# A list schedule rebuilt: new durations with margins, 22 activation groups, work moved to VectorE, identity products in TensorE's early waits, the last tile by rows

## The chip, the cores and the metric

One core of one Trainium2 chip. The metric is the device time of the slowest (here the only) core in microseconds. Every comparison below is between executions that were put in the fast state; executions of one kernel scatter by 2 to 4 us to either side of their median (the kernel before: 530.85 to 536.88 us in 63 runs on one chip), and its medians on the chips used here lie between 532.2 and 533.0 us. So ratios are always taken against the kernel before on the same chip in the same rounds.

## The reference, cut to what matters

```python
# 4 sequences of 5824 steps, 256 channels: a gated linear recurrence ...
a_t   = exp(8 * sigmoid(r_gate) * log(sigmoid(a_param)))
x_in  = sqrt(max(1 - a_t*a_t, 1e-6)) * sigmoid(i_gate) * x
h     = a_t[:, t] * h + x_in[:, t]          # over t, y[:, t] = h
# ... and on its 23296 rows a multiplicative feed-forward net (w3: 1024 x 1024)
out   = ((y @ w1) * (y @ w2)) @ w3 @ w_out
```

## The kernel before

The rows are cut into chunks: one of 256, then 45 of 512. Per chunk, ScalarE takes tanh of both gates, the decay's exp and a square root; the gates are turned by TensorE (first chunks) or by transposing DMAs; GpSimd and VectorE make products and squares; VectorE scans; then four pairs of "up" tiles (pa, pb) on TensorE, a copy of pa by ScalarE, the product g by VectorE, four "down" tiles, a copy out and a store. w3 and w_out are folded into one matrix wp at the start. Square root needs another activation table than tanh and exp, so chunks are taken in groups: all roots of a group stand together.

The order of instructions is not written by hand. A list scheduler in the kernel's own Python gives every piece of work (a job) an engine, a duration, a due date and buffers, lets time run, and each time an engine is free picks the ready job with the earliest due date. Only the resulting order reaches the chip: each engine executes its instructions strictly in that order.

```python
group_sizes = [2, 2, 2, 3, 3, 4, 4, 4, 4, 3, 4, 2, 5, 4]
NPE, NDV, NCV = 6, 4, 8      # chunks turned by TensorE; products, squares by VectorE; casts by VectorE
WCE = {'w1': 'POOL', 'w2': 'POOL', 'wo': 'POOL', 'w3': 'DVE'}     # who casts the weights
BACKLOG = 0.5                # bulk loads wait while more than this many us of DMA are queued
DUE_W, DUE_W3, LAG = -4.0, 20.5, 21.5                              # ... and a dozen more due dates

def copy(c, mp):   nc.scalar.copy(out=sa, in_=T["pa", c, mp])       # cut
def evac(c, j2):   nc.scalar.copy(out=T["ot", c, j2], in_=T["po", c, j2])
def root(c):       nc.scalar.activation(out=n, in_=n, func=AF.Sqrt, scale=-1.0, bias=1.0)

job(("copy", c, mp), "ACT", 0.15 + 0.82 * f, t + 0.9, ...)          # engine, duration, due date
BUFS = {"pab": 3, "po": 2, "g": 3, "sa": 3, "rt": 2, "th_r": 2, ...}

while any(waiting.values()):                                        # cut
    for e in free:
        key = choose(e, t)        # first ready job of this engine by due date
        ...
        done[key] = end; order.append((start, len(order), key))
for _, _, key in sorted(order):
    jobs[key]["fn"]()             # emit in the order of the planned starts
```

## Time and profile before

| | before |
|---|---|
| time, median of 3 (range) | 532.49 us (532.16 to 533.09) |
| span of the profiled execution | 530.9 us |
| busy: TensorE, VectorE, ScalarE, GpSimd | 498.4, 446.7, 463.1, 335.8 us |
| activation table loads | 31 |
| end of TensorE's work to end of the span | 4.2 us |

TensorE is the engine to look at, and its own work doesn't change with the schedule, so what a schedule does to the time is read from TensorE's *lost* time. The prediction below counts it from blocks. For comparisons I count it in one way for all kernels: TensorE loads weights for every tile and all these loads are in the trace, in order. From one tile's first weight load to the next I subtract the tile's work (0.867 us for a full up, down or fold product tile, 0.445 for eight transposes; halves for chunk 0; 488.6 in all, the identity products counting as nothing). What remains is lost. For the kernel before that gives 34.0 us lost by 84.7 us and 38.1 in all. The prediction's block count splits the same 38.0 as 36.2 and 1.8. That split is wrong: it counts up tiles by their copies and products, which come later than the tiles. By the matmuls' own starts, 28 full up tiles and not 26 began before 84.7 us, so 34.6 us were lost before and 3.5 after; the sum is the same.

### The profile page before, as it was taken

What the parts mean: (1) busy time and instruction counts of PE and PEld (TensorE: products, weight loads), DVE (VectorE), ACT (ScalarE), POOL (GpSimd) and SP (SyncE); (2) the same over time, 40 slices, a digit from 0 to 9 for tenths busy, and PEclk for the clock granted to TensorE, in tenths of its full rate; (3) what the DMA queues carried; (4) which work ended last, traced back from release to release, by engine and by line L of the source; (5) the groups of instructions that cost most, each with busy time, mean ns of one, the idle gap of its engine ahead of it and who ended that gap; (6) DMA issues with size and microseconds to landing.
All of it is one profiled execution on the core that took longest, in us unless ns stands there. A gap on an engine that the chain in (4) does not pass through costs nothing.

```text
span 530.9 us, 8667 instructions
## 1 busy us (share of the span) xinstructions
PE 498.4 (94%) x3144; PEld 303.3 (57%) x3144; DVE 446.7 (84%) x367; ACT 463.1 (87%) x546; POOL 335.8 (63%) x260
## 2 busy tenths in 40 slices
PE   1568899999999999999999999999999999999997
PEld 1434565666565566565656565565665655566655
DVE  2998988997968899998999988789898889899641
ACT  6998879999999999999999899799998999965452
POOL 1338485887758686876859788578868578841000
PEclk9999999999999999999999999999999999999999
DMA  8998999999997996997997879999899787231112
GB/s 274 356 359 243 292 282 296 324 299 275 295 273 199 279 315 171 278 299 197 287 252 221 226 204 238 329 196 266 226 274 303 199 208 212 61 98 59 41 61 99
DMA packets 184939, 124.31 MB, mean 234 GB/s; under 512 B 88640, under 2 KB 182848, under 8 KB 184896
## 3 DMA queue, kind: packets, MB, share of 16 engines
q1 hardware_dynamic: 184624, 123.76, 86.4%
q8 instruction: 24, 0.39, 0.3%
q14 instruction: 19, 0.16, 0.1%
q10 hardware_dynamic: 272, 0.00, 0.0%
HBM read 78.91 MB, written 23.86 MB: 194 GB/s over the span
## 4 chain that ended last, share of the span: by engine, by line
PE 81%; DVE 8%; ACT 4%; issue 3%; DMA 3%; SPq 0%; DVEq 0%; ACTq 0%
PE pa L227 27%; PE pb L227 26%; PE po L248 26%; DVE g_t L241 2%; DMA rt<-th_r 2%; DVE h_t L211 2%; DVE w_t L276 1%; ACT sa L234 1%; PE pw L299 1%; ACT th_i L133 1%; DMA i_t<-in_i_gate_dram 1%; DVE nrm L196 1%; DVE u_t L148 1%; ACT ot L254 1%; ACT a_t L179 1%
## 5 line engine op out<-in xcount | busy, mean ns | idle before, releaser
L241 DVE TENSOR_TENSOR g_t<-sa,pb 128x1024 bf16<-128x1024 bf16 (+1 forms) x184 | 218.4, 1199 | 60.0 <-ACT sa L234 44.8
L227 PEld LDWEIGHTS <-w_sb 128*128 128x128 bf16 x1472 | 144.6, 98 | 149.1 <-issue 10.7
L234 ACT CAST sa<-pa 128x1024 bf16<-128x1024 f32 (+1 forms) x184 | 183.0, 999 | 32.8 <-PE pa L227 30.9
L227 PE MATMUL pa<-y_t,w_sb 128*128 128x512 bf16 (+1 forms) x736 | 188.7, 380 | 4.0 <-DVE g_t L241 4.0
L227 PE MATMUL pb<-y_t,w_sb 128*128 128x512 bf16 (+1 forms) x736 | 188.4, 379 | 2.9 <-DVE g_t L241 1.5
L248 PE MATMUL po<-wp_sb,g_t 128*128 128x256 bf16 x1456 | 181.7, 273 | 0.2 <-DVE nrm L196 0.2
L248 PEld LDWEIGHTS <-g_t 128*128 128x128 bf16 x1456 | 142.4, 98 | 46.0 <-issue 0.4
L211 DVE TENSOR_TENSOR_SCAN h_t<-a_t,h_t,nrm 128x512 f32<-128x512 f32 (+3 forms) x90 | 136.6, 1534 | 0.8
L187 POOL TENSOR_TENSOR nrm<-a_t 128x512 f32<-128x512 f32 x84 | 104.7, 1258 | 43.5 <-ACT a_t L179 43.2
L153 POOL TENSOR_TENSOR u_t<-th_i,x_t 128x512 bf16<-128x512 f32 x80 | 116.5, 1472 | 2.5
L219 POOL CAST y_t<-h_t 128x1024 bf16<-128x1024 f32 x38 | 44.6, 1173 | 67.9 <-DVE h_t L211 62.1
L138 POOL TENSOR_SCALAR th_i<-th_i 128x1024 f32<-128x1024 f32 x42 | 57.6, 1371 | 21.8 <-ACT th_i L133 21.8
L254 ACT COPY ot<-po 128x512 f32<-128x512 f32 x91 | 53.4, 587 | 16.3 <-PE po L248 15.6
L179 ACT ACTIVATE a_t<-rt,la 128x512 f32<-128x512 bf16 x80 | 63.5, 816 | 4.5 <-DMA rt<-th_r 4.2
L196 DVE SCALAR_TENSOR_TENSOR nrm<-nrm,ut 128x1024 f32<-128x1024 f32 x40 | 59.8, 1494 | 2.4 <-ACT nrm L191 2.4
L133 ACT ACTIVATE th_i<-i_t 128x1024 f32<-128x1024 f32 (+1 forms) x46 | 48.2, 1052 | 1.1 <-DMA i_t<-in_i_gate_dram 1.0
L191 ACT ACTIVATE nrm<-nrm 128x1024 f32<-128x1024 f32 (+1 forms) x46 | 48.1, 1056 | 0.8 <-DVE nrm L187 0.6
L126 ACT ACTIVATE th_r<-r_t 128x1024 bf16<-128x1024 f32 x40 | 42.3, 1063 | 2.1 <-DMA r_t<-in_r_gate_dram 2.0
L161 PE MATMUL ptr<-ident,th_r 128*128 128x128 bf16 x44 | 4.7, 269 | 16.7 <-DVE ident L73 8.7
L276 POOL CAST w_sb<-wf 128x1024 bf16<-128x1024 f32 x4 | 6.1, 1545 | 19.7 <-DMA wf<-in_moe_w_dram 19.7
L191 ACT ACT_TABLE_LOAD x14 | 18.0, 1283 | 0.2
L161 PEld LDWEIGHTS <-th_r 128*128 128x128 bf16 x44 | 3.7, 122 | 18.5 <-ACT th_r L124 14.9
(33 smaller groups left out, 127.1 us busy)
## 6 DMA issues: line engine op xcount, KB each, us to landing
out_dram<-ot SPq DMA_DIRECT2D x91, 256.0 KB, 3.6
r_t<-in_r_gate_dram SPq DMA_DIRECT2D x45, 512.0 KB, 5.3
i_t<-in_i_gate_dram SPq DMA_DIRECT2D x45, 512.0 KB, 5.2
x_t<-in_x_dram SPq DMA_DIRECT2D x45, 512.0 KB, 5.0
wf<-in_moe_w_dram SPq DMA_DIRECT2D x12, 512.0 KB, 5.7
wf<-in_moe_w_out_dram SPq DMA_DIRECT2D x2, 512.0 KB, 6.0
rt<-th_r SPq DMA_TRANSPOSE x40, 4.5
ut<-u_t SPq DMA_TRANSPOSE x40, 4.6
```

Source lines behind the costliest of these rows:

```text
L138: nc.gpsimd.tensor_scalar(t, t, 1.0, 1.0, op0=ALU.add, op1=ALU.mult)
L153: nc.gpsimd.tensor_mul(out=u.rearrange("p cb j q -> p j cb q")[:, js], in0=cut(t)[:, js], in1=cut(T["x", c])[:, js])
L179: nc.scalar.activation(out=T["a", c][:, cb, :w], in_=T["pr", c][:, cb, :w], func=AF.Exp, scale=la4[:, cb:cb + 1], bias=la4[:, cb:cb + 1])
L187: eng.tensor_mul(out=T["n", c][:, cb, :w], in0=T["a", c][:, cb, :w], in1=T["a", c][:, cb, :w])
L191: nc.scalar.activation(out=T["n", c][:, :, :w], in_=T["n", c][:, :, :w], func=AF.Sqrt, scale=-1.0, bias=1.0)
L196: nc.vector.scalar_tensor_tensor(out=T["n", c][:, :, :w], in0=T["n", c][:, :, :w], scalar=1e-3, in1=T["pu", c][:, :, :w], op0=ALU.max, op1 ...
L211: nc.vector.tensor_tensor_scan(T["h", c][:, cb, lo:hi], T["a", c][:, cb, lo:hi], T["n", c][:, cb, lo:hi], init, ALU.mult, ALU.add)
L227: nc.tensor.matmul(out=pp[:, q, :w], lhsT=w_sb[:, cb, m * P:(m + 1) * P], rhs=T["y", c][:, cb, :w], start=(cb == 0), stop=(cb == NCB - 1))
L234: nc.scalar.copy(out=sa[:, :, :w], in_=T["pa", c, mp][:, :, :w])
L241: nc.vector.tensor_mul(out=T["g", c][:, 2 * mp:2 * mp + 2, :w], in0=T["sa", c, mp][:, :, :w], in1=T["pb", c, mp][:, :, :w])
L248: nc.tensor.matmul(out=T["po", c, j // 2][:, j % 2, :], lhsT=T["g", c][:, k, j * P:(j + 1) * P], rhs=wp_sb[:, k, :], start=(k == 0), stop= ...
L254: nc.scalar.copy(out=T["ot", c, j2], in_=T["po", c, j2])
```

## The change

Its intent: replace the due dates by a schedule searched on durations recorded on the chip, with a margin added to each, so that the order also holds when jobs are late; let smaller groups shorten the lead; give VectorE some of ScalarE's copies; use TensorE's early waits for products with the identity matrix, whose results nobody reads, to bring its clock up; and shorten the tail. The arithmetic and all buffers stay. Cut to its core:

```diff
-    group_sizes = [2, 2, 2, 3, 3, 4, 4, 4, 4, 3, 4, 2, 5, 4]
+    group_sizes = [2, 1, 1, 2, 3, 3, 2, 3, 2, 1, 1, 2, 5, 3, 3, 1, 2, 3, 2, 2, 1, 1]
-    NPE = 6 ; NDV = 4 ; NCV = 8
+    TURN_R = {0, 1, 2, 3, 5, 6, 10} ; TURN_U = {0, 1, 2, 3, 4}
+    DV_TIMES = {0, 1, 3, 4} ; DV_SQUARE = {0, 1, 3, 4, 5} ; DV_CAST = {2, 3, 4, 7, 10, 11, 13}
+    DV_EVAC = {1, 7, 14, 15, 16, 18, 21, 25, 30, 32, 33, 35, 42, 43, 44}
+    DV_COPY = {4, 16, 18, 19, 20, 23, 25, 29, 32, 33, 34, 42, 43, 44}
-    WCE = {'w1': 'POOL', 'w2': 'POOL', 'wo': 'POOL', 'w3': 'DVE'}
+    W_CAST = {"w1": "DVE", "w2": "POOL", "wo": "POOL", "w3": "POOL"}
-    BACKLOG = 0.5
+    BACKLOG = 1.75
+    M_OCC, M_LAT, M_PE = 0.06, 0.038, 0.0055          # margins on every job
+    OFFSET = {"r": -20.0, "i": -7.5, ...} ; SHIFT = {("w3", 0): 36.0, ...}   # some 240 due dates, chunks 0 to 13
 def up(c, mp, nm, w_sb):
+        for _ in range(warm.get((nm, c, mp), 0)):
+            nc.tensor.matmul(out=pp[:, 0, :P], lhsT=ident, rhs=ident, start=True, stop=True)
 def copy / evac:
+        copy_to(mp == 0 and c in DV_COPY, ...)   /   copy_to(c in DV_EVAC, ...)
 def down(c, j):
+        if c == NCH - 1:
+            T["po_last", j] = po = psum_o.tile([P, D], F32, name="po", tag="po")   # then evac_last, store_last per row tile
 ...
-                job(("copy", c, mp), "ACT", 0.15 + 0.82 * f, t + 0.9, ...)
+                job(("copy", c, mp), e, o + s * f, o + s * f + (0.115 if e == "DVE" else 0.15), t + 0.9, ...)
 ...
+            if key[0] in ("pa", "pb") and t < WARM and t - free[e] > 0.25:
+                n = int((t - free[e]) * 0.8 / 0.0556)
+                if n > 3:
+                    warm[key] = min(n, 60)
```

## The prediction

> **What bounds the kernel now.** I read the page's busy shares first, then the busy times of every engine in eight stretches, the groups of instructions in the two stretches that matter, the waits, and last the order in time of the first and last 30 us.
>
> ```profile
> span 530.9 us, 8667 instructions
> PE 498.4 (94%) x3144; PEld 303.3 (57%) x3144; DVE 446.7 (84%) x367; ACT 463.1 (87%) x546; POOL 335.8 (63%) x260
> 0.00:20.70 20.70, 3.85 (x32) 3.26 (x33) 10.30 (x15) 15.92 (x19) 3.98 (x8) 1.00 0.94 301
> 20.70:84.70 64.00, 54.95 (x395) 34.01 (x393) 58.81 (x58) 55.07 (x69) 40.99 (x32) 0.97 1.01 303
> 84.70:200.00 115.30, 114.93 (x710) 69.47 (x710) 102.06 (x80) 110.64 (x132) 82.82 (x63) 1.00 1.06 281
> 460.00:519.00 59.00, 58.98 (x361) 35.27 (x361) 43.72 (x36) 32.58 (x38) 11.78 (x10) 1.00 0.20 60
> ```
>
> In the last four lines the columns are the stretch, its length, the busy us of PE, PEld, DVE, ACT and POOL, the granted clock, DMA share and GB/s. TensorE is full from 84.7 us on; only the first 85 us are not. But a matmul's end is modelled, so I count work instead. In the steady part a block (four products of 512 columns for an up tile, or eight of 256 for a down tile) starts every 0.867 us: in the order of time, three of them (pa, pb, po) repeat every 2.60 us up to 519. From 84.7 us to the last product's start plus its share (526.8) the groups of that stretch hold 167 copies of pa, 167 products and 87 output copies, so 167+167+174 = 508 blocks, 508 x 0.8667 = 440.3 us in 442.1 us. Only **1.8 us are lost in the last 442 us**; no schedule can take more than that from there.
>
> Before 84.7 us TensorE did: chunk 0's eight half tiles 3.5; 26 full up tiles 22.5; 8 down tiles 6.9; the weight fold, 8 x (0.44+0.87) = 10.5; 12 transposes at 0.445 (half for chunk 0) 5.1. Sum 48.5 us. So **36.2 of the first 84.7 us are lost**, and 4.1 after the last matmul (526.8 to 530.9). Floor of pure work: 48.5+440.3 = 488.8; check: 488.8+36.2+1.8+4.1 = 530.9.
>
> ```profile
> 8.72 0.59 PE L161 MATMUL ptr<-ident,th_r 128*128 128x128 bf16 x4 [8.72 <-DVE ident L73]
> 19.91 1.03 PE L161 MATMUL ptr<-ident,th_r 128*128 128x128 bf16 x8 [4.96 <-ACT th_r L124]
> 20.73 1.06 PE L227 MATMUL pa<-y_t,w_sb 128*128 128x256 bf16 x4
> 29.31 0.60 PE L227 MATMUL pa<-y_t,w_sb 128*128 128x256 bf16 x4
> 37.67 1.86 PE L227 MATMUL pa<-y_t,w_sb 128*128 128x512 bf16 x4 [1.70 <-DVE g_t L241]
> ```
>
> Columns: start, length, engine, line, what it does, count, idle time before and its releaser. The same four products take 1.06 us at 20.73 and 0.60 at 29.31, and the 512-wide ones 1.86 at 37.67 against 1.03 later: TensorE is at half speed after its long waits. By the starts of the following tiles I put this at 3.5 us in all. So the 36.2 us are: 18.9 before the first up tile (20.7 less 1.8 of transposes), 3.5 of half speed, 13.8 of waits from 20.7 to 84.7.
>
> In that ramp VectorE is 58.81 of 64.0 us busy and ScalarE 55.07: together they are the limit, not DMA latency (few DMA waits of ScalarE are in it), and not TensorE.
>
> ```profile
> L241 DVE TENSOR_TENSOR g_t<-sa,pb 128x1024 bf16<-128x1024 bf16 x180 | 215.7, 1210 | 59.9 <-ACT sa L234 44.8 <-PE pb L227 10.3 <-ACT ot L254 2.1
> ...
> L234 ACT CAST sa<-pa 128x1024 bf16<-128x1024 f32 x180 | 180.8, 1009 | 32.6 <-PE pa L227 30.8 <-DVE g_t L241 0.5
> ...
> L211 DVE TENSOR_TENSOR_SCAN h_t<-a_t,h_t,nrm 128x512 f32<-128x512 f32 x84 | 130.1, 1566 | 0.7
> ...
> L254 ACT COPY ot<-po 128x512 f32<-128x512 f32 x91 | 53.4, 587 | 16.3 <-PE po L248 15.6
> ...
> L191 ACT ACT_TABLE_LOAD x14 | 18.0, 1283 | 0.2
> ...
> L276 DVE CAST w_t<-wf 128x1024 bf16<-128x1024 f32 x8 | 8.7, 1105 | 0.0
> ```
>
> After the bar: busy us, mean ns of one, then the idle time before and its releasers. The 60 us that VectorE waits at g_t lie where TensorE is full: they are slack, not loss.
>
> **What the Trainium skill says.** "TensorE: Matmul & The Clock Gate", section "What's actually happening": half clock after an idle window, full clock after about 3.4 us of sustained work. The trace agrees in kind: 0.85 us between starts of the 256-wide tiles at 20.7, 0.43 at 29.3. "ScalarE: Activation LUTs", section "Table sets: the hidden batching unit": tanh and exp share a set, sqrt needs another; the trace has 31 loads of 1283 ns for 14 groups, two per group and three at the start (14+7+6+3+1 in the groups). "SBUF — State Buffer", section "SBUF: two separate sides": VectorE with two SBUF inputs and GpSimd exclude each other for a whole instruction. The trace agrees: the scan takes 1566 ns on average, and 1277 in the last 46 us where GpSimd has little left. So moving work to GpSimd is not free for VectorE's scans and gates.
>
> **The change, part by part.**
>
> 1. Schedule. The arithmetic is the same; the due dates, groups and engine of each job change. TensorE's 488.8 us stay (12 transposes before: 6+6; after: 7+5).
> ScalarE: 15 chunks' output copies go to VectorE, 30 x 0.587 = -17.6; 14 pa copies go, 14 x 1.009 = -14.1; 22 groups in place of 14, two loads each, 16 x 1.283 = +20.5. Net -11, to about 452 us.
> VectorE: 30 output copies at an estimated 0.6 (half the width of the 1.21 product), +18; 14 copies at about 1.2, +17; w3 casts to GpSimd, -8.7; two w1 casts, +1.4; one more chunk of squares, +2.3; casts nearly even. Net about +30, to about 476 us.
> None of this gives TensorE time after 84.7; it only makes VectorE tighter (476 in a span near 520 is 92%).
>
> 2. The ramp, where the gain is. VectorE loses there the w3 casts (-8.7) and the casts of chunks 0, 1, 5 and 6 (0.42 + 3 x 0.69 = -2.5) and gains w1 casts (1.4), squares (2.3), chunk 1's output copies and chunk 4's copy (2.4): -5.1. ScalarE: by 84.7 the old order had tanh done for chunks 0 to 9 with up tiles only into chunk 4, a lead of nearly six chunks, because whole groups of 2, 2, 2, 3 must pass the square root together. A chunk of lead costs ScalarE 2 x 1.06 + 2 x 0.8 + 1.06 = 4.8 us. Groups 2, 1, 1, 2, 3 need perhaps two chunks less by then: -9.6, less one more pair of loads (+2.6) : -7. Both engines are thus relieved by 5 to 7 us, and the 5 and 9 us that they idle in the ramp can be cut by better order. I take 8 of the 13.8 us of waits.
>
> 3. Start. The identity's cast is queued first, and chunk 0's transpose needs no longer wait for it until 8.72. But ScalarE has hardly a gap from 4.5 to 16.4 (tanh, rates, three table loads, exp, then the root of the first group, still two chunks), so the first root stays near 15. The old order then put chunk 1's gate (18.21) ahead of chunk 0's scan result being cast (19.33) and a cold transpose (19.91) ahead of the first up tile. I take 1.5 us, first up tile near 19.2. The preloaded log set replaces a load that was there anyway: 0.
>
> 4. Identity products. Up to 60 in a planned wait over 0.25 us in the first 80 us, filling 80% of it at 0.0556 us each, the full-speed spacing. They bring TensorE to full speed: of the 3.5 us I take 2.5. At half speed they last twice as long (0.107), so a filled wait can overrun by 0.6 of itself; and where the wait is for a PSUM buffer, they too wait for it and come on top. I take 0.5 us back for that, inside the 8 above.
>
> 5. Last tile by rows. Its copy of 256 columns (0.38, as wp's copy from pw) instead of 0.58, and a store of half the size, estimated 0.3 less: -0.5 of the 4.1.
>
> Sum: first part 36.2-8-1.5-2.5 = 24.2; middle 1.8 to 3 (tighter VectorE, more groups); end 3.6. Span 488.8+24.2+3.0+3.6 = 519.6. The time is 1.6 above the span (532.49 against 530.9): **521.2 us**, 2.1% less. As a search over hundreds of due dates probably finds some more than my averages, I put it at **520.5 us**.
>
> **The rivals.**
> - VectorE becomes the bound in the middle. For it: +30 us, scans stretched by GpSimd, three pab buffers only, so a late product stops TensorE within two tiles. Against it: 60 us of slack at g_t, and output and pa copies are given to it where the plan saw room. If half of the chunks cost 0.3 us each, +7: about 527.
> - The ramp stays bound by ScalarE (more table loads among the first chunks) and only the order changes: 3 us in place of 8, so about 526, within 2%.
> - The plan comes out nearly as meant: it gives 11 of the 13.8 us of waits back, first up tile at 18, middle as clean as before. Then about 514.
> - Identity products overrun in several waits: +2 to +4 on any of these.
>
> **Range and chances.** 8 in 10: 512 to 527. The threshold of 2% is 521.8 us, just above my figure, so the chances are close: faster 0.58, same 0.39, slower 0.03. Slower would need more than 10 us of new stalls in a kernel that loses 42 in all, with the schedule chosen to withstand delays.
>
> **What would show it.** First up tile near 19 us; TensorE's full stretch beginning near 70 to 75 instead of 85; lost time before it near 24 us; no 1.8 us up tile in the first 60 us; under 4 us lost after it; VectorE near 476 and ScalarE near 452 us busy, 47 table loads; 3.6 us from last matmul to end. I am wrong if TensorE's waits on g_t or sa spread through 100 to 460 us, if the first up tile is still at 20.7, or if the products with the identity stand ahead of up tiles whose input had long been ready.

## The result, and the profile after

The changed kernel took **537.31 us** (536.72 to 539.00, 4 runs) beside 532.79 us for the kernel before: a ratio of 1.009, 95% interval 1.0061 to 1.0118. So it is not 2.3% faster but 0.9% slower, outside my range of 512 to 527. (A ratio is the mean time of one kernel's fast runs over that of the other's of the same rounds, so not quite the ratio of the medians that I quote.) The profiled execution was the slowest of the four; a second study of the same kernel, told below, gave 1.013.

From the page of the changed kernel (span 537.2 us): busy time and share of each engine, and the shares of the chain that ended last; after it the same chain line of the kernel before.

```profile
PE 500.6 (93%) x3165; PEld 309.2 (58%) x3221; DVE 472.6 (88%) x408; ACT 450.1 (84%) x515; POOL 353.2 (66%) x265
...
PE 60%; ACT 14%; DMA 11%; issue 7%; DVE 7%; SPq 1%; POOL 0%; ACTq 0%; DVEq 0%; POOLq 0%
```

```profile
PE 81%; DVE 8%; ACT 4%; issue 3%; DMA 3%; SPq 0%; DVEq 0%; ACTq 0%
```

The busy times are nearly what I had worked out (VectorE 476 forecast, 472.6 measured; ScalarE 452 and 450.1). What they did to TensorE is not. Of the chain that ends the kernel, TensorE's share fell from 81% to 60%: ScalarE and DMA took its place.

Now the ramp. Busy time by engine (PE, PEld, DVE, ACT, POOL) in three stretches, then the granted clock, DMA share and GB/s; the kernel before first, then the changed one.

```profile
20.00:40.00 20.00, 15.84 (x102) 9.49 (x103) 19.77 (x20) 18.66 (x23) 7.67 (x7) 0.94 1.08 361
40.00:60.00 20.00, 16.55 (x132) 10.10 (x131) 18.55 (x19) 17.04 (x21) 12.89 (x11) 0.98 0.89 276
60.00:80.00 20.00, 18.85 (x144) 12.59 (x142) 17.94 (x17) 15.38 (x21) 15.81 (x13) 1.00 1.04 269
```

```profile
20.00:40.00 20.00, 18.97 (x157) 13.67 (x157) 18.39 (x19) 18.87 (x23) 12.27 (x12) 1.00 1.09 356
40.00:60.00 20.00, 18.08 (x157) 12.11 (x159) 19.76 (x20) 15.45 (x22) 11.11 (x10) 1.00 1.15 299
60.00:80.00 20.00, 13.74 (x106) 9.86 (x106) 14.91 (x14) 18.03 (x22) 17.13 (x12) 0.91 1.11 325
```

Up to 60 us the new order is ahead (identity products swell its PE figures, so go by lost time: 28.0 us against 31.5). From 60 to 80 us it gives back more than it had won: TensorE is busy 13.74 us instead of 18.85, and the lost time grows by 8.8 us against 2.0. The chain of work in that stretch shows one part of it (start, length, what):

```profile
51.99 6.87 DMA rt<-th_r
...
58.88 1.53 ACT a_t L246 x2
...
61.87 1.28 ACT L263
...
63.17 1.07 ACT nrm L263
...
68.12 1.33 DVE nrm L268
69.45 1.99 DVE h_t L283
...
71.46 1.35 DVE y_t L291
72.81 1.97 DVE h_t L283
74.78 0.59 DVE ot L308
...
75.42 2.64 PE po L333 x12
```

A transposed th_r lands after 6.87 us, exp waits for it, then a table load and the root, then gates, scans and a cast on VectorE in a row, and only behind them, in VectorE's queue, an output copy that frees the buffer which a down tile needs. In this execution the moved output copy put TensorE behind VectorE's longest jobs. The down tiles after the wait ran at half speed besides (16 products from 75.42 us on took 3.49 us; 16 took 1.91 in the kernel before).

The chain leaves out another wait in the same stretch. The change also gave the w3 casts to GpSimd, and TensorE waited for them. Its waits (us in all, how many, the longest) in this profile, then in the second one of the same kernel, told below:

```profile
PE ptw L379 <- POOL w_t L370: 3.1, 3, 2.1
PE po L333 <- DVE ot L308: 2.7, 1, 2.7
```

```profile
PE ptw L379 <- POOL w_t L370: 4.2, 4, 2.1
PE po L333 <- DVE ot L308: 0.6, 1, 0.6
```

In the kernel before, TensorE waited 1.3 us for VectorE's w3 casts. So the wait for GpSimd's casts comes back in the second profile, and the long wait for an output copy does not.

Where all of the 6.3 us between the two profiled spans came from, by lost time:

| lost, us | before | after | difference |
|---|---|---|---|
| by 60 us | 31.5 | 28.0 | -3.5 |
| 60 to 84.7 us | 2.5 | 8.8 | +6.3 |
| after 84.7 us | 4.1 | 8.4 | +4.3 |
| tail, last tile's work to end | 4.2 | 3.4 | -0.8 |

After 84.7 us ScalarE waits longer for transposed th_r, which take longer to land. The waits (us in all, how many, the longest), the kernel before and then the changed one:

```profile
ACT a_t L179 <- DMA rt<-th_r: 4.2, 5, 2.1
```

```profile
ACT a_t L246 <- DMA rt<-th_r: 14.2, 10, 4.7
```

and the lines of DMA issues (median us from issue to landing last), in the same order:

```profile
rt<-th_r SPq DMA_TRANSPOSE x40, 4.5
```

```profile
rt<-th_r SPq DMA_TRANSPOSE x39, 5.7
```

From 215 to 275 us, where 2.8 us are lost, that transpose is 40.4% of the chain in the changed kernel, and TensorE (its po, pa, pb) hardly in it.

There is one more reading, which needs no chip and which I had left out. The scheduler computes an end for every job, so each kernel carries the end that its schedule expects: the largest entry of `done` when its code has run. For the kernel before it is 526.3 us, for the changed one 529.4, with the first up tile at 20.1 and 22.0 us. By its own reckoning, margins included, the new schedule was never earlier. TensorE's lost time can be counted on the planned starts as on measured ones. By 84.7 us it is 32.2 us in the plan before and 32.2 us in the new plan (33.9 and 36.8 in all). So the 12 us that I forecast for the ramp were not in the plan that was to bring them, and of the 8.8 us lost between 60 and 80 us the plan itself has 4.8. The rest came on the chip: by 84.7 us the changed kernel lost 4.6 us more than its plan (2.7 in the second profile), the kernel before 1.8.

### The profile page after: what moved, and what is told of

It reads as the page before. It is cut to its first block, busy times and chain, and to the rows that moved or that the text cites. A ratio compares the mean times of both kernels' runs of the same rounds, so it can differ in the third digit from the quotient of the medians.

```text
span 537.2 us, 8765 instructions
## 1 busy us (share of the span) xinstructions
PE 500.6 (93%) x3165; PEld 309.2 (58%) x3221; DVE 472.6 (88%) x408; ACT 450.1 (84%) x515; POOL 353.2 (66%) x265
## 4 chain that ended last, share of the span: by engine, by line
PE 60%; ACT 14%; DMA 11%; issue 7%; DVE 7%; SPq 1%; POOL 0%; ACTq 0%; DVEq 0%; POOLq 0%
PE po L333 20%; PE pb L302 19%; PE pa L302 19%; DMA rt<-th_r 9%; ACT sa L310 4%; ACT a_t L246 2%; DVE g_t L322 2%; ACT th_i L199 2%; ACT L263 2%; DVE h_t L283 2%; DMA r_t<-in_r_gate_dram 2%; ACT th_r L192 1%; DVE nrm L268 1%; DMA i_t<-in_i_gate_dram 1%; ACT nrm L263 1%
## 5 line engine op out<-in xcount | busy, mean ns | idle before, releaser
L322 DVE TENSOR_TENSOR g_t<-sa,pb 128x1024 bf16<-128x1024 bf16 (+1 forms) x184 | 218.2, 1198 | 34.5 <-ACT sa L310 18.4
L310 ACT CAST sa<-pa 128x1024 bf16<-128x1024 f32 (+1 forms) x170 | 168.0, 997 | 37.7 <-PE pa L302 36.1
L302 PE MATMUL pa<-y_t,w_sb 128*128 128x512 bf16 (+1 forms) x704 | 183.0, 377 | 5.4 <-DVE g_t L322 2.5
L254 POOL TENSOR_TENSOR nrm<-a_t 128x512 f32<-128x512 f32 x82 | 114.0, 1407 | 20.9 <-ACT a_t L246 20.6
L220 POOL TENSOR_TENSOR u_t<-th_i,x_t 128x512 bf16<-128x512 f32 x82 | 123.2, 1520 | 1.5
L291 POOL CAST y_t<-h_t 128x1024 bf16<-128x1024 f32 (+1 forms) x39 | 51.1, 1309 | 95.1 <-DVE h_t L283 86.3
L246 ACT ACTIVATE a_t<-rt,la 128x512 f32<-128x512 bf16 x78 | 61.1, 813 | 14.4 <-DMA rt<-th_r 14.2
L204 POOL TENSOR_SCALAR th_i<-th_i 128x1024 f32<-128x1024 f32 x42 | 52.3, 1246 | 11.8 <-ACT th_i L199 11.8
L268 DVE SCALAR_TENSOR_TENSOR nrm<-nrm,ut 128x1024 f32<-128x1024 f32 x41 | 54.4, 1328 | 2.2 <-ACT nrm L263 1.1
L310 ACT COPY ot<-po 128x512 f32<-128x512 f32 (+1 forms) x61 | 35.4, 582 | 23.2 <-PE po L333 22.9
L308 DVE COPY ot<-po 128x512 f32<-128x512 f32 (+1 forms) x32 | 21.2, 666 | 6.8 <-PE po L333 6.8
L308 DVE CAST sa<-pa 128x1024 bf16<-128x1024 f32 x14 | 17.0, 1213 | 0.5 <-PE pa L302 0.3
L228 PE MATMUL ptr<-ident,th_r 128*128 128x128 bf16 x52 | 5.1, 254 | 10.5 <-ACT th_r L190 10.2
```

Of the source, the lines that this page charges most:

```text
L204: nc.gpsimd.tensor_scalar(t, t, 1.0, 1.0, op0=ALU.add, op1=ALU.mult)
L220: nc.gpsimd.tensor_mul(out=u.rearrange("p cb j q -> p j cb q")[:, js], in0=cut(t)[:, js], in1=cut(T["x", c])[:, js])
L246: nc.scalar.activation(out=T["a", c][:, cb, :w], in_=T["pr", c][:, cb, :w], func=AF.Exp, scale=la4[:, cb:cb + 1], bias=la4[:, cb:cb + 1])
L254: eng.tensor_mul(out=T["n", c][:, cb, :w], in0=T["a", c][:, cb, :w], in1=T["a", c][:, cb, :w])
L268: nc.vector.scalar_tensor_tensor(out=T["n", c][:, :, :w], in0=T["n", c][:, :, :w], scalar=1e-3, in1=T["pu", c][:, :, :w], op0=ALU.max, op1 ...
L302: nc.tensor.matmul(out=pp[:, q, :w], lhsT=w_sb[:, cb, m * P:(m + 1) * P], rhs=T["y", c][:, cb, :w], start=(cb == 0), stop=(cb == NCB - 1))
```

## The experiments

Experiments on a list schedule need care: change a duration or a set, and the whole order comes out anew. So most edits below act after the schedule is made: the order stays frozen, and only the engine, the function or the transfer of some jobs is changed. A frozen order says what a relief is worth in that order, not what an order made anew for it could reach. "Lost" is as above, from each run's one profiled execution, which can lie up to 2.3 us from the median (b_w3pool: 534.5 against 532.2). The changed kernel itself gave 1.009 on one chip and 1.013 on another, and lost 36.8 and 34.9 us by 84.7 us. So a smaller difference than some 2 us from it is not clear of noise.

| run | median us | ratio to before | lost by 84.7 | lost in all |
|---|---|---|---|---|
| before | 532.5 | | 34.0 | 38.1 |
| changed | 537.3 | 1.009 | 36.8 | 45.2 |
| after_again | 540.0 | 1.013 | 34.9 | 46.4 |
| a_allact | 542.8 | 1.020 | 35.9 | 48.5 |
| a_notab | 535.9 | 1.007 | 37.1 | 42.2 |
| a_lightdma | 534.1 | 1.004 | 35.9 | 40.8 |
| a_noplus | 537.9 | 1.012 | 36.6 | 43.2 |
| a_nofold | 531.2 | 0.997 | 41.9 | 48.4 |
| a_nowarm | 535.4 | 1.006 | 35.1 | 42.9 |
| a_notab_foldc | 535.1 | 1.004 | 34.9 | 41.2 |
| a_port | 534.7 | 1.003 | 34.4 | 40.6 |
| a_light_notab | 534.8 | 1.004 | 37.9 | 42.6 |
| b_nofold | 529.9 | 0.994 | 42.0 | 44.9 |
| b_lightdma | 530.3 | 0.996 | 34.2 | 37.0 |
| b_small | 532.7 | 0.999 | 32.4 | 37.5 |
| b_small_foldc | 534.8 | 1.003 | 36.1 | 41.3 |
| b_moves | 539.7 | 1.012 | 35.3 | 46.5 |
| b_w3pool | 532.2 | 0.999 | 35.4 | 39.9 |
| b_groups | 540.8 | 1.015 | 41.9 | 46.7 |
| b_searched | 532.7 | 0.999 | 32.0 | 37.5 |

(a_: the changed kernel with the edit; b_: the kernel before with the edit. The two nofold kernels have 10.5 us less of TensorE's work.)

### Four suspects in the changed order

The copies go back to ScalarE:

```diff
+    DV_EVAC = set() ; DV_COPY = set()        # after the schedule is made
```

> The changed kernel in its own frozen order; only the 30 output copies and 14 pa copies that it gave to VectorE are executed by ScalarE at the same places of the order. Theory B (VectorE, 30 us more loaded, makes TensorE wait): the time falls by 3 us or more towards 533, and the 3.5 us gap before the down tile near 77 us goes. Theory A (the chain tanh, transposing DMA, exp is too late) and theory F (ScalarE is short of time): the same or slower by 0 to 6 us, since ScalarE gets some 32 us of work back while VectorE loses 38.

Measured 542.8 us, 1.020. Between 60 and 80 us 6.5 us are lost instead of 8.8 (the unchanged kernel's second profile has 5.9, so this shows nothing), but afterwards more was lost than ever, 12.6 us: by the waits view VectorE's products now wait 55.3 us for ScalarE's copies (18.4 in the changed kernel). In this order, made for 22 groups, ScalarE has no room for them. Theory B as a repair is out; that the moves cost something is not, and comes back below.

No table loads; the root is computed with exp, so the result is wrong:

```diff
-    func=AF.Sqrt
+    func=AF.Exp
```

> Wrong result on purpose: the root is computed with exp, which needs no other table, so about 44 table loads of 1.283 us (56 us of ScalarE) vanish; order and all else as in the changed kernel. Theory F (ScalarE's 22 groups with two loads each are what TensorE waits for): the time falls by 6 us or more, below 531. Theory A (DMA latency in the chain to exp): a fall of 1 to 3 us, with ScalarE still waiting over 10 us for transposed th_r. Theory E (the port that VectorE and GpSimd share): under 2 us.

535.9 us. Three table loads of 44 remain, ScalarE is busy 52 us less (398.2 instead of 450.1), and the median is 1.4 us lower, by ratios 0.2 to 0.6%. The loss by 84.7 us is 37.1, unchanged, though ScalarE is busy 10 us less there (60.4 instead of 70.2; a later expectation says 15, which is wrong); after it, 5.1 instead of 8.4. In this order ScalarE's time alone isn't what the ramp waits for. ScalarE's waits for transposed th_r stay, 16.3 us. Theory A's figures fit, F is out.

The loads of x from chunk 8 on left out (38 of the 138 loads of gates and x; bytes read fall by a quarter, from 78.9 to 59.0 MB), so the result is wrong:

```diff
 def load(c, nm):
+        if nm == "x" and c >= 8:
+            T[nm, c] = T[nm, 7]
+            return
```

> Wrong result on purpose: chunks from 8 on take x from chunk 7's tile, so 38 loads of 512 KB are gone; order otherwise as in the changed kernel. Theory A (transposed th_r lands late because bulk loads fill the DMA engines): median time from issue to landing of th_r's transposes falls from 5.7 to under 4 us, ScalarE's wait for them from 14.2 to under 4 us, and the time falls by 4 us or more, to 533 or less; what is lost before 84.7 us hardly changes. Theories B, E and F: under 1.5 us.

534.1 us, 3.2 less than the changed kernel. Transposes of th_r land after 4.5 us (not under 4), ScalarE waits 4.2 us for them instead of 14.2, and 4.9 us are lost after 84.7 instead of 8.4; by 84.7 us hardly anything changes. The mechanism is right, the gain a little under the forecast.

GpSimd without the addition of 1 (wrong result):

```diff
 def plus(c):
+        if c >= 8:
+            return
```

> Wrong result on purpose: from chunk 8 on GpSimd does not add 1 to th_i, which takes 1.0 us of 8 us of its work per chunk away; order otherwise as in the changed kernel. Theory E (VectorE's scans and gates and all of GpSimd's work exclude each other and together take nearly the 10.4 us that TensorE needs per chunk): the time falls by 4 us or more and scans shorten from 1.61 us. Theories A, B and F: under 1.5 us.

537.9 us: nothing, although the scans went from 1606 to 1514 ns. Theory E is out for the later part.

> Wrong result on purpose, control for the same cut in the changed kernel, where it gave 3 us: chunks from 8 on take x from chunk 7's tile. If late transposes are what the changed kernel's order is sensitive to and the order before is not, this one gains under 1.5 us. If it gains 3 us as well, DMA load is a cost that both orders share and it doesn't explain the difference.

The control, the same cut in the kernel before: 530.3 us, 0.996. I expected under 1.5 us and got about 2.2. So DMA load costs both orders something; the changed order feels it more (0.5 to 0.9% against 0.4%), and 0.1 to 0.5%, or 0.5 to 2.7 us, of the difference can be put down to it, not 4; the intervals don't tell the lower end from nothing.

### Is the ramp bound by the fold?

In both kernels the last fold ends near 69 us and the first down tile starts at 69 us. With three g buffers, up tiles can't run far ahead without down tiles. That looked like the bound of the ramp:

```diff
 for _, _, key in sorted(order):
+        if key[0].startswith("fold") or "w3" in key:
+            continue                          # and the down tiles use w_out as it is: wrong result
```

> Wrong result on purpose: the eight w3 pieces are not loaded, cast or folded, and the down tiles use w_out as it is; the order of all else is the changed kernel's. TensorE's own work falls by the fold's 10.5 us. Theory G (the first down tile waits for the last fold near 69 us in both kernels, and with three g buffers the up tiles stop after chunk 2 until then, so the fold sets the end of the first stage): TensorE's lost time falls besides, from 36.8 us at 84.7 us to under 29, and the time by 18 us or more, to 519 or less. Theory H (VectorE, ScalarE and their shared chain bound the ramp, as the prediction had it): only the 10.5 us and some 2 for the relief of VectorE and GpSimd, so about 524 to 527.

> The same removal in the kernel before, in its own order. Theory G: from 532.2 down by 18 us or more, to 514 or less. Theory H: by 10 to 13 us, to 519 to 522.

531.2 and 529.9 us. Theory G falls, clearly: 10.5 us of TensorE's own work taken out of the ramp brought 2.9 us in the kernel before and some 6 in the changed one. The rest turned into waiting: in the kernel before the first down tile starts 9.4 us earlier (59.8 instead of 69.2), and then TensorE waits, 3.6 us of it for ScalarE's output copy. The same 28 up tiles stand ahead of the first down tile as before, since the order is frozen; an order made without the fold was not tried. Busy time of the kernel before without its fold, from 20.7 to 84.7 us:

```profile
20.70:84.70 64.00, 50.57 (x281) 27.72 (x284) 49.78 (x45) 55.51 (x65) 41.94 (x32) 0.89 0.85 251
```

VectorE is busy 49.78 of 64 us there, ScalarE 55.51, GpSimd 41.94, DMA 85%: no engine is full, and TensorE has lost 42.0 us all the same. Theory H, with VectorE and ScalarE as the bound, forecast 10 to 13 us and is not right either.

### Relief in the ramp, engine by engine

ScalarE takes VectorE's eight copies of w3t, without table loads (wrong result); then, instead of that, GpSimd is relieved (no additions from chunk 2 on, w3 casts by ScalarE, again without table loads):

```diff
+    FOLD_C = "ACT"                            # after the schedule is made; func=AF.Exp as above
```

> Wrong result on purpose. The run without table loads showed that ScalarE's 15 us of relief before 84.7 us left TensorE's loss there unchanged (37.1 us against 36.8). Here ScalarE also takes VectorE's eight copies of w3t (5.4 us). Theory V (VectorE's queue is what the ramp waits for): the loss at 84.7 us falls to 34 or less and the time by 3 us or more against the run without table loads (535.9), to 533 or less. Theory L (the ramp waits for latencies along one chunk's chain of steps, not for an engine's time): less than 1.5 us.

```diff
 def plus(c):
+        if c >= 2:
+            return
 def cast_w(key, dst, eng):
+            eng = "ACT"                       # for w3; func=AF.Exp as above
```

> Wrong result on purpose. As without table loads, and GpSimd is relieved from the start: no addition of 1 to th_i from chunk 2 on, w3 casts by ScalarE; that is some 13 us less of GpSimd's work before 84.7 us and 42 after. Theory P (GpSimd's work stretches VectorE's scans, gates and casts, since they exclude each other; that ate the relief which I had predicted): the loss at 84.7 us falls from 37.1 to 34 or less, casts by VectorE from 1288 to under 1000 ns, scans from 1.61 to under 1.45 us, time 531 or less. Otherwise: 534 to 536.

535.1 and 534.7 us. The loss by 84.7 us fell from 37.1 to 34.9 and 34.4: less than each theory asked for (2.2 and 2.7 us; the two profiles of the unchanged kernel differ by 1.9). VectorE's casts took 1191 ns with GpSimd relieved (not under 1000; 1101 without table loads alone), the scans 1511 (not under 1450). Even with ScalarE and GpSimd this free, the changed order loses more than the order before does with all its work.

The same kind of relief in the order before, done with parts of the change itself. First the two small parts, then the copies of w3t to ScalarE on top of them, then the w3 casts to GpSimd alone:

```diff
+    nc.vector.tensor_copy(out=ident, in_=ident_f)      # first of VectorE's queue
+    # last tile: po, copy and store for each of its four row tiles   (b_small)
+    FCA = True                                          # b_small_foldc
+            eng = "POOL"                                # for w3: b_w3pool
```

> The kernel before in its own order, with two small parts of the change: the identity is cast ahead of VectorE's other work, and the last tile is copied and stored row by row. The wait of 8.7 us for the identity at the start is not what the first up tile waits for, as ScalarE runs without a gap from 4.5 to 16.4 us; the tail was 4.2 us before and 3.4 after the change. So 0.5 to 1.3 us less: 531.2 to 532. If neither is worth anything here: the same within 0.4.

> As the run before it, with the eight copies of w3t by ScalarE instead of VectorE. Theory V: VectorE's 5.2 us of relief in the ramp gives 2 us or more over the run before it. Theory L: under 1 us. If ScalarE, which idles 8.9 us in the ramp, becomes late itself: slower.

> The kernel before in its own order, only with the eight w3 casts on GpSimd instead of VectorE. By my prediction this relieves VectorE of 8.7 us in the ramp and should give about half of it: 528 to 530. If GpSimd is then late itself, as it executes squares and products in between, or stretches VectorE's instructions: 532 to 536, with VectorE's busy time before 84.7 us down by less than 6 us.

532.7 us (0.9994, interval 0.9973 to 1.0015), 534.8 and 532.2. The small parts shorten the tail from 4.2 to 3.4 us, and the time says the same as before within its interval. Relieving VectorE by 5 us did not help but cost 2 us, since TensorE then waited for ScalarE (3.3 us for w3t). Relieving it of the w3 casts:

```profile
20.70:84.70 64.00, 54.00 (x387) 35.43 (x393) 52.63 (x50) 54.91 (x69) 48.84 (x39) 0.95 1.00 300
```

VectorE 52.63 us busy instead of 58.81, and the time 0.9991, no change that can be told from none; TensorE waited 3.5 us for GpSimd's casts instead. This is a step that I had counted on, tried here in the old order.

### The two large parts, each alone in the kernel before

Only the moved copies, in the frozen order; then only the groups, for which the old scheduler builds its order anew:

```diff
+    if mp == 0 and c in DV_COPY: nc.vector.tensor_copy(...)     # b_moves
+    if c in DV_EVAC:             nc.vector.tensor_copy(...)
```

> The kernel before in its own order, only with the change's 30 output copies and 14 pa copies on VectorE instead of ScalarE. VectorE gets 38 us more (446.7 to about 485), ScalarE 32 us less. If these moves by themselves cost TensorE time: slower by 2 us or more. If ScalarE's room is worth more than VectorE's load: faster by 1 us or more. TensorE lost only 4.1 us after 84.7 us in this order, so there is little to win and more to lose: I expect 534 to 538.

```diff
-    group_sizes = [2, 2, 2, 3, 3, 4, 4, 4, 4, 3, 4, 2, 5, 4]    # b_groups
+    group_sizes = [2, 1, 1, 2, 3, 3, 2, 3, 2, 1, 1, 2, 5, 3, 3, 1, 2, 3, 2, 2, 1, 1]
```

> The scheduler before with the change's 22 groups, everything else of it as before; its order is built anew, and the end that the schedule computes for itself is 535.6 us (526.3 before; 529.4 for the changed kernel, of which the profiled run took 537.2 against 530.9 before). If that end tells the measured time: 540 or more. If groups don't matter on the chip and the schedule's own end says little: 531 to 536.

539.7 us, 1.012 (slower than I expected), and 540.8 us, 1.015. They fail in different places. The moves leave the ramp about as it was and lose **11.2 us after 84.7 us instead of 4.1**. From 84.7 to 530 us:

```profile
84.70:530.00 445.30, 435.07 (x2628) 261.28 (x2676) 400.75 (x335) 364.85 (x417) 293.53 (x223) 1.00 0.84 219
```

VectorE is busy 400.75 of 445.3 us there, 90% (85% in the kernel before), ScalarE 82%; TensorE's waits in that stretch are for VectorE's g_t (4.2 us), its sa copies (1.6) and ScalarE's sa (0.9). Here a share of 90%, with long jobs of another kind in the same queue, was enough for TensorE to run dry. The groups do the opposite: **41.9 us lost by 84.7 us instead of 34.0**, and 4.8 after. Their table loads before 84.7 us are as many as before (10), so it isn't loads that they cost in the ramp; it is the order that comes out of them. And its own expected end, 535.6 us against 526.3, had said so: measured span 539.5. Most of the loss in the ramp is in its plan too: 37.8 us by 84.7 us, against 32.2.

### What remained

The identity products taken out:

```diff
+    warm.clear()                              # after the schedule is made
```

> The changed kernel in its own order without its 77 identity products. Theory C (they hold up the tiles behind them: 31 of them take from 19.6 to 22.9 us, just ahead of the first up tile): the first up tile starts by 21.5 and the time falls by 1 us or more. Rival: they only use waits and raise the clock; without them up tiles near 23 us run at half speed and the time is the same within 0.7 us or longer.

535.4 us, 1.006 against 1.009 and 1.013 with them. The first up tile starts at 22.0 us instead of 22.8 and runs at half speed: by 30 us, 21.7 us are lost without and 21.8 with them. At this place they are worth nothing. TensorE's order in the changed kernel (start, length, what, count):

```profile
18.79 1.01 PE L228 MATMUL ptr<-ident,u_t 128*128 128x128 bf16 x8 [1.62 <-DVE nrm L268]
19.60 3.51 PE L298 MATMUL pa<-ident 128*128 128x128 bf16 x31
22.90 1.06 PE L302 MATMUL pa<-y_t,w_sb 128*128 128x256 bf16 x4
23.76 0.89 PE L302 MATMUL pb<-y_t,w_sb 128*128 128x256 bf16 x4
24.48 0.60 PE L302 MATMUL pa<-y_t,w_sb 128*128 128x256 bf16 x4
```

All 31 run at half speed (3.51 us, 0.11 each), overrun the wait, and the first up tile is still at half speed. The time is 0.3 to 0.7% better without them, with a scatter of 6 us in 17 runs; its profile loses less between 60 and 80 us (7.2 us against 8.8), but the second profile of the changed kernel, with the products, has 5.9 there. So I leave it open.

Both cuts, loads and tables, together, to see what is left after 84.7 us:

> Wrong result on purpose: the changed kernel's order with both the x loads from chunk 8 on and the square root's table loads gone. Alone, they took 3.1 and 1.4 us off. If the losses after 84.7 us are ScalarE waiting for late transposes without room to catch up, the loss there falls to 4.5 us or less (8.4 in the changed kernel, 4.1 before) and the time to 533 or less, with the loss before 84.7 us still near 36. If something else is left: more than 6 us lost after 84.7 us.

534.8 us, 4.7 us lost after 84.7: near the 4.5 that I had set, and hardly less than each cut gave alone (4.9 and 5.1). This reads as one loss with two cures, not two losses: ScalarE must have room when the transposed th_r is late, or it must not be late. The time is 1.8 us above the limit that I had set, with 37.9 us lost by 84.7.

The changed kernel once more, and a search with the old scheduler for an earlier end of its own, with the two small parts:

> The changed kernel unchanged, for a second profile. If the split of its loss is its own and not that of one slow execution: 35 to 38 us lost before 84.7 us and 6.5 to 9 after, against 34.0 and 4.1 in the kernel before; time 535 to 539.

> The scheduler before with other due dates, another grouping from chunk 9 on and NCV 11, found by searching for the earliest end that the schedule gives itself (525.3 against 526.3), with the identity cast first and the last tile stored by rows. If that end is a guide to 1 us: 1 to 2 us faster than before, 531 to 532. If it only ranks schedules several us apart: within 2 us either way.

540.0 us, 1.013: the changed kernel is slower, on a second chip too. By 84.7 us it lost 34.9, just under my band, but 2.1 us followed at 92, so that by 100 us it is 37.1, against 36.8 in the first profile and 34.5 in the kernel before; in all 46.4 against 38.1. The split at 84.7 us is thus uncertain by some 2 us; that it loses in both parts is not. The searched schedule gave 532.7 us, 0.999 (0.9975 to 1.0005): the same. An expected end that is 1 us earlier is not a guide to 1 us; ends 3 and 9 us later did go with slower kernels (1.009 and 1.013; 1.015), though the second study doesn't tell these two apart. No version with the right result beats the kernel before by an amount that can be told from none.

## Why the prediction was wrong

Step by step, by its own numbers:

- *TensorE's work stays at 488.8 us, and the busy times of the whole span.* Right: VectorE +26 us (I said +30), ScalarE -13 (-11), 44 table loads (I said 47).
- *The last tile by rows, -0.5.* Right in kind: 4.2 to 3.4 us. In the kernel before, with the identity cast, it can't be told from nothing in the time.
- *The start, first up tile near 19.2.* Wrong: 22.8. The new order loads chunk 1's r and chunk 0's x ahead of chunk 0's i, which lands at 7.5 us instead of 5.3. From there ScalarE works on with hardly a gap, for as long as in the old order, and the first root starts at 17.4 instead of 15.2. I took the order's improvement for granted, without looking for the order.
- *Identity products, 2.5 of the 3.5 us of half speed.* Wrong: nothing gained by 30 us. I had named the overrun at half speed, and that is what happened to 31 of the 77.
- *The ramp, 8 of 13.8 us of waits.* **This is the step that failed.** Of the 17.6 us between the forecast span (519.6) and the measured one (537.2), 14.8 lie in the ramp with its start: I forecast 12 us less lost there and 2.8 more were (0.9 more in the second profile). Three things in the step were wrong. First, the better order was assumed: the plan loses 32.2 us there, as the old one does. Second, the relief came short: by 84.7 us VectorE was busy 65.2 us instead of 69.1 (-3.9; I said -5.1), and ScalarE 70.2 instead of 71.0 (-0.8; I said -7), as tanh of r had still been done for 11 chunks (10 before) and of i for 8 (10 before), with 11 table loads instead of 10. Third, I read VectorE at 58.81 and ScalarE at 55.07 of 64 us as the bound, so that 5 to 7 us less work would give time. In a frozen order it does not: 6.2 us off VectorE gave nothing in the kernel before, 10 us off ScalarE by 84.7 us left the changed kernel's ramp where it was, and 10.5 us off TensorE itself gave 2.9. Two reliefs together gave 2.2 and 2.7 us, about the difference between two profiles of one kernel. What the ramp waits for is a chain that crosses five in-order queues for each chunk, each step behind other chunks' jobs. That is argued from the exclusion of single engines and fits the chain of 52 to 78 us shown above; it has not been shown by a run of its own, and stays open. The lead that smaller groups were to save (-9.6 us of ScalarE) was the other half of this step: alone, in the old scheduler, they lose 7.9 us more by 84.7 us.
- *The middle, 1.8 to 3.* Wrong in size: 4.1 to 8.4 by one count for both (11.4 in the second profile; and 1.8 was itself miscounted, 3.5 by the matmuls' starts). I had the rival (VectorE as the bound, about +7) and called the 60 us that VectorE waits at g_t "slack". They are slack as a sum. The moves alone, in an order that did not need them, lost 7.1 us more after 84.7 us. In the changed kernel a late DMA adds to it: about 3.5 us of its 8.4 go when the DMA engines have a quarter fewer bytes to read, or when ScalarE has 52 us more room.
- *The range.* It held the improvement fixed and let only its size vary; I gave 0.03 to "slower by 2%" because the schedule was "chosen to withstand delays". The chances for *same* (0.39) were the only part that met the result.

What stays open: how the changed kernel's own loss divides between groups, moves and due dates. Its order was made with all of them at once; taking the moves back in it made it worse, and each alone in the other order is not the same thing.

## What to carry to other kernels

When every engine executes a fixed order and several are 85 to 95% busy, an engine's busy share does not say what its relief is worth: freeze the order, relieve one engine at a time, and believe only that, for that order. Before building a rearranged schedule, compare the end that it expects of itself with that of the old one, count TensorE's lost time in both plans, and look up when the first dependent work can start in it. Don't put copies that free TensorE's buffers into a queue behind the longest jobs of another stage, even where that queue has idle time in sum.

## What the Trainium skill lacked or had wrong

- "Perfetto Trace Analysis", section "Identifying the Most-Contended Engine", says to find the engine with the highest occupancy and to optimize it first. In the ramp that was VectorE (58.81 of 64.0 us), and taking 6.2 us off it changed the time by a ratio of 0.9991. What the page does not give is the worth of relieving one engine in a fixed order across several in-order queues, where no engine is full (VectorE 78%, ScalarE 87%, GpSimd 66% of the ramp without the fold) and TensorE still waits.
- "TensorE: Matmul & The Clock Gate", section "What's actually happening", gives some 3.4 us of sustained work until full clock. Here TensorE ran from 18.79 us without a visible gap, and its spacing fell from 0.213 to 0.110 us per 256-wide product only near 24.3, 5.5 us later. The section lets the moment vary by 0.5 us, since its window runs freely; the other 1.6 us are not explained here. The page says nothing on whether products issued into a wait pay for themselves; here they did not (21.8 us lost by 30 us with them, 21.7 without).
- "SBUF — State Buffer", section "SBUF: two separate sides", has the exclusion between VectorE and GpSimd, but no size for a mix such as this one: the 512-wide scan took 1606 ns in the changed kernel, 1514 with 1 us per chunk less on GpSimd, and 1277 in the kernel before's last 46 us, where GpSimd had little left.
- No page has that a transposing DMA's time to landing depends on the bulk loads beside it: median 5.7 us, 4.5 with a quarter fewer bytes read, in the same order (4.5 and 3.9 in the kernel before).
